# Batch 3's q and k turned by transposing transfers instead of by TensorE

## The chip, the cores and the metric

The kernel runs on one core of a Trainium2 chip. The metric is the time of one execution on the device in microseconds (us). A core has TensorE (matrix products, with a queue of its own for loading weights), VectorE, ScalarE, GpSimd and SyncE; in the profile's lines they are PE and PEld, DVE, ACT, POOL and SP. DMA transfers are issued by SyncE and GpSimd, at the end by ScalarE too.

## The reference

The inputs q, k and v have 8 batches, 8 heads, 576 positions and 64 elements; s has one number for each batch, head and position. The kernel computes causal attention with a bias from the running sum of s, and a mixer behind it:

```python
scores = scale * np.matmul(q, k.transpose(0, 1, 3, 2))
cum = np.cumsum(np.maximum(s, 0.0), axis=-1)
bias = -(cum[:, :, :, None] - cum[:, :, None, :])
scores = np.where(causal, -1000000000.0, scores + np.minimum(bias, 0.0))
attn = softmax(scores)                     # over the last axis
x = matmul(attn, v), heads side by side    # (8, 576, 512)
u = x + (x.transpose(0, 2, 1) @ U @ V).transpose(0, 2, 1)
out = u + np.maximum(u @ w_ch1, 0.0) @ w_ch2
```

For the scores, q and k of a head must lie with their 64 elements on the partitions, while they come from memory with the positions in rows. So each must be turned, and that is what the change is about.

## The kernel before

**Pairs.** The heads are taken two at a time: pair n holds two heads of batch n // 4, and there are 32 pairs (NP), four to a batch (PB). For each pair the program makes the turned q and k with the rows of the bias (a "slot" of 68 partitions: 64 of q or k and 4 of bias), then scores(n) (products at L441, exponentials on ScalarE at L459, L471 and L477, masks on VectorE at L385), then values(n) (products with v at L505; on VectorE a reciprocal at L514 and the scaled result into x_sb at L515; a transposing transfer of x_sb into xT at L522). Three slots are used in turn, so the bias rows of pair n (rows_of, L305, on SyncE) wait for the scores of pair n - 3.

**Two ways of turning.** ZB = 4 says which batches go which way. For batches 0 to 3, load(b) brings q and k of a whole batch with few large transfers on GpSimd (L132 or L137), into qk_sd0 and qk_sd1 in turn (batch b into qk_sd[b % 2]). transposes(n) turns a pair on TensorE: 16 transposes at L325, eight for each head, into two PSUM buffers of the pool pwork. Four copies (L345 from batch 2's second half on, L348 before) move them into the slot, by parity of the run; copies() puts a few of them on ScalarE. For batches 4 to 7, load_pair(n) brings one pair with four transfers on GpSimd (L124), turn_pair(n) turns it with one transposing transfer on SyncE (L365) into a landing place, and part_pair(n) copies it into the slot with one VectorE copy for each head (L375). There are three landing places: a tile of its own ("turned"), a part of qk_sd0 behind the pairs, and the front of qk_sd1.

**The order.** The loop at L1255 takes n from 8 on. Step n does, as far as each exists: loads of a later batch, turn_pair(n + 3), load_pair(n + 7), the turning of pair n + 1 (transposes or part_pair), scores(n), values(n - 1), loads of v (L188). Between the pieces, step_fill() puts pieces of the mixer: chanmix, with products at L675 into pwork, ScalarE's ReLU at L1052, sums at L711 and L260 on VectorE, products at L733, additions at L747; seqmix(b), with products at L535 that read all of batch b's x_sb, goes between the pieces of step 4b + 5. The order on TensorE and GpSimd is that of the program (L1333). On VectorE, ScalarE and SyncE a scheduler may move instructions; placed() (L907) ties a copy at L375 to the VectorE instruction that the program has before it, and `after(tc, last_sp(), x_turned[-1])` (L369) ties a turn on SyncE behind the latest transposing transfer of x.

**What waits for what on the queues.** Each engine takes its instructions in order. A turn waits until its pair is loaded and its landing place has been copied out; a load of a later pair into the same place waits for the turn. pwork is a pool of four PSUM buffers that the transposes, parts of the scores, values and the mixer take in turn.

Of the kernel before, what the change touches and what calls it, by code (L numbers as in the profile page):

```python
# [19 lines left out]
def after(tc, ins, prev):  # L20
    tc.add_manual_dep(
        ins,
        prev.name,
        mybir.DependencyInfo(mybir.DependencyClass.NoSync, mybir.DependencyReason.DATA),
        reason="in_program_order",
    )
# [15 lines left out]
def kernel(  # L42
# [23 lines left out]
    NP = BH // 2  # L66
    PB = NP // B
# [2 lines left out]
    KA = D + 4  # L70
    NF = FF // 128
    FT = 2
    ZB = 4
    TR, RT = 96, 6

    consts = ctx.enter_context(tc.tile_pool(name="consts", bufs=1))
# [35 lines left out]
    def of_pair(n):  # L112
        return qk_sd[ZB % 2][:TR, ds(n % PB * QK // PB, QK // PB)].rearrange(
            "p (c t two d) -> p c t two d", c=2, t=RT, two=2
        )
# [4 lines left out]
    def load_pair(n):  # L120
        b, hp = divmod(n, PB)
        for hh in range(2):
            for c, src in enumerate((q, k)):
                nc.gpsimd.dma_start(  # L124
                    out=of_pair(n)[:, c, :, hh, :],
                    in_=src[b, 2 * hp + hh].rearrange("(t p) d -> p t d", p=TR),
                )
# [54 lines left out]
    def load_v(b, parts=range(5)):  # L182
        vt = v_slot(b)
        if 0 < b < 3:
            init_v(nc.gpsimd, vt)
        for t in parts:
            rows_t = 128 if t < 4 else 64
            nc.gpsimd.dma_start(  # L188
                out=vt[:rows_t, t, :, 0:D],
                in_=v[b, :, ds(t * 128, rows_t), :].rearrange("h p d -> p h d"),  # L190
            )
# [161 lines left out]
    landings = [consts.tile([128, 2 * S], BF16, name="turned")]  # L353
    landings += [qk_sd[ZB % 2][:, ds(QK, 2 * S)], qk_sd[(ZB + 1) % 2][:, 0 : 2 * S]]

    def landing(n):
        return landings[(n - ZB * PB) % 3]

    x_turned = []

    def last_sp():
        return [ins for ins in list(nc.cur_bb.bb.instructions) if ins.engine == E.SP][-1]

    def turn_pair(n):
        nc.sync.dma_start_transpose(  # L365
            out=landing(n).rearrange("p (a m) -> p a m", m=TR),
            in_=of_pair(n).rearrange("p c t two d -> p (c t two d)"),
        )
        after(tc, last_sp(), x_turned[-1])  # L369

    def part_pair(n):
        rows_of(n)
        for hh in range(2):
            placed(
                lambda: nc.vector.tensor_copy(  # L375
                    slot_of(n)[0:D, hh, 0 : 2 * S], landing(n)[ds(hh * D, D)]
                )
            )
            yield
# [57 lines left out]
    def scores(n, pT, spins=()):  # L437
        slot = slot_of(n)

        def mm(dst, hh, j, lo, hi):  # L440
            nc.tensor.matmul(  # L441
                dst,
                lhsT=slot[0:KA, hh, ds(S + j * 128, 128)],
                rhs=slot[0:KA, hh, lo:hi],
                start=True,
                stop=True,
            )

        tail = None
        if spins:  # L450
            tail = pwork()
            spin(spins[0], tail)
        for hh in range(2) if n > 0 else ():
            near = pscore()
            for j in range(4):
                mm(near[:, ds(j * 128, 128)], hh, j, j * 128, j * 128 + 128)
            mm(near[:, 512:960], hh, 0, 128, S)
            mm(near[:, 960:1024], hh, 3, 512, S)
            nc.scalar.activation(pT[:, hh, 0:1024], near, EXP, scale=scale)  # L459
            if n >= PB:  # L460
                mask(pT[:, hh, 0:512].rearrange("p (a b) -> p a b", a=4), 4, 128)
            if spins:
                spin(spins[1 + hh], tail)
            yield
        mid, tail = pscore(), tail if spins else pwork()
        for hh in range(2):
            mm(mid[:, ds(hh * 512, 320)], hh, 1, 256, S)
            mm(mid[:, ds(hh * 512 + 320, 192)], hh, 2, 384, S)
            if spins and hh == 0:
                spin(spins[3], tail)  # L470
        nc.scalar.activation(  # L471
            pT[:, :, 1024:1536], mid.rearrange("p (a b) -> p a b", a=2), EXP, scale=scale
        )
        yield
        for hh in range(2):
            mm(tail[:, ds(hh * 64, 64)], hh, 4, 512, S)
        nc.scalar.activation(  # L477
            pT[:, :, 1536:1600],
            tail[:, 0:128].rearrange("p (a b) -> p a b", a=2),
            EXP,  # L480
            scale=scale,
        )
        if n >= PB:
            mask(pT[:, :, 1536:1600], 2, 64)
        yield
# [606 lines left out]
    def step_fill():  # L1092
        pace[0] += pace[1]
        if pace[0] < 16:
            return
        pace[0] -= 16
        if NG - 3 in expanded and not ps_tail:
            return
        while fill:
            if next(fill[0], fill) is not fill:  # L1100
                return
            fill.pop(0)

    def run(gen):
        for _ in gen:
            step_fill()
# [5 lines left out]
    def fill_with(n):  # L1112
        per, pace[1] = pace[1], 16
        for _ in range(n):
            step_fill()
        pace[1] = per


    def pT_of(n):
        if n < PB + 3:  # L1120
            return pTs[n % 2] if n % PB < 2 else pT_early[n % PB - 2]
        return pTs[(n + 1) % 2]

    def step(*gens):
        for gen in gens:
            next(gen, None)
# [85 lines left out]
    def load(b):  # L1212
        alloc_qk(b)
        for h in range(0, H, 4 if b == 2 else H):
            load_qk(b, h, 4 if b == 2 else H)
# [39 lines left out]
    for n in range(2 * PB, NP + 2):  # L1255
        b, hp = divmod(n, PB)
        if hp == 0 and b + 1 < ZB:
            load(b + 1)
        if ZB * PB <= n + 3 < NP:
            turn_pair(n + 3)  # L1260
        if n + 5 == ZB * PB:
            for m in range(ZB * PB, (ZB + 1) * PB):
                load_pair(m)
        if (ZB + 1) * PB <= n + 7 < NP:
            load_pair(n + 7)
        mixing = seqmix(b - 1) if hp == 1 and b > FT else iter(())
        if b == B:
            fill_with(3)
            for _ in range(3):
                step(mixing)  # L1270
                fill_with(2)
        if n > 2 * PB and n + 1 < NP:
            for at, _ in enumerate((transposes if n + 1 < ZB * PB else part_pair)(n + 1)):
                step_fill()
                if at == 0:
                    step(mixing)
        if 2 * PB + 1 < n < NP:
            for at, _ in enumerate(scores(n, pT_of(n))):
                step_fill()
                if at == 1:  # L1280
                    step(mixing)
        for _ in mixing:
            fill_with(1)
        if hp == 1 and FT < b < B:
            fill.append(chanmix(b - 1))
            pace[1] = 12 if b < 6 else 10
        if 2 * PB < n <= NP:
            run(values(n - 1, pT_of(n - 1)))
        if 2 <= b < B - 1:
            if b + 1 < ZB:  # L1290
                load_v(b + 1, range(5 if hp == 0 else 0))
            else:
                load_v(b + 1, ((0, 1), (2,), (3,), (4,))[hp])
# [70 lines left out]
```

## Time and profile before

| | us |
|---|---|
| median of 3 runs | 353.72 (353.6 to 353.72) |
| the profiled execution | 353.81 |
| its span | 352.1 |
| TensorE busy | 341.3 |
| VectorE busy | 264.3 |
| ScalarE busy | 207.5 |
| GpSimd busy | 113.2 |

The granted TensorE clock was 0.999 in this execution. The span is what the trace covers; 1.7 us of the execution lie around it. A group's line gives the source line, engine and operation, output and inputs, shapes and count, then the busy time and the mean length in ns, then the idle time of the engine before them and what ended it. A line of the chain gives start, length and the work that the end of the kernel hung on. A line of a timeline gives start, length, engine, line, operation and tiles, and in brackets the idle time before it with what ended that. A transfer's line shows when it was issued, not when its data came.

### The profile page before, as it was taken

How to read it: one execution, taken by the hardware profiler on the slowest of the kernel's cores; microseconds unless marked ns; L12 is line 12 of the kernel's file. 1: busy time of each engine (PE TensorE's matmuls, PEld its weight loads, DVE VectorE, ACT ScalarE, POOL GpSimd, SP SyncE). 2: the span in 40 equal slices, each digit the busy share in tenths (PEclk: the TensorE clock that was granted, in tenths of full speed). 3: DMA queues.
4: the chain of work that ended last, by engine and by line, in shares of the span. 5: the costliest groups of instructions: out<-in, count | busy, mean ns of one | idle time of the engine just before them, and what ended most of it. 6: DMA issues, size and time to landing. Idle time of an engine off the chain costs nothing.

```text
span 352.1 us, 9157 instructions
## 1 busy us (share of the span) xinstructions
PE 341.3 (97%) x3735; PEld 248.6 (71%) x3770; DVE 264.3 (75%) x584; ACT 207.5 (59%) x314; POOL 113.2 (32%) x158
## 2 busy tenths in 40 slices
PE   8999999999999999999999999999899999999996
PEld 4685566666588756885688567866587558888885
DVE  8686776778797857985699549974888588775774
ACT  4795975747763577347743785368562545675710
POOL 8898373534724047244634456000000000000000
PEclk9999999999999999999999999999999999999999
DMA  7999999999949999999999999784034333010022
GB/s 101 154 198 205 182 185 135 145 146 141 132 41 120 176 141 128 133 120 199 136 133 123 203 135 149 125 156 93 0 69 101 89 67 85 30 61 32 30 91 89
DMA packets 163713, 42.06 MB, mean 119 GB/s; under 512 B 148312, under 2 KB 162040, under 8 KB 163672
## 3 DMA queue, kind: packets, MB, share of 16 engines
q0 software_dynamic: 101744, 18.45, 77.8%
q1 hardware_dynamic: 61640, 22.83, 35.4%
q8 instruction: 29, 0.48, 0.6%
q10 hardware_dynamic: 288, 0.20, 0.2%
q14 instruction: 12, 0.10, 0.1%
HBM read 37.25 MB, written 9.70 MB: 133 GB/s over the span
## 4 chain that ended last, share of the span: by engine, by line
PE 82%; DVE 10%; ACT 5%; issue 3%; DVEq 0%; ACTq 0%
PE pwork L675 23%; PE pwork L733 13%; PE quarter L733 10%; PE pscore L441 9%; PE pwork L505 7%; PE parts L963 6%; PE pwork L694 3%; PE pwork L325 2%; ACT pT L459 2%; DVE uT L560 2%; DVE slot L348 2%; ACT hT L1052 2%; PE pscore L216 1%; DVE slot L711 1%; PE pscore L402 1%
## 5 line engine op out<-in xcount | busy, mean ns | idle before, releaser
L675 PE MATMUL pwork<-uT,w_sb 128*128 128x512 bf16 x405 | 104.4, 379 | 2.5 <-ACT hT L1052 0.9
L1052 ACT ACTIVATE hT<-pwork 128x512 bf16<-128x512 f32 x108 | 65.4, 611 | 37.0 <-PE pwork L675 36.1
L459 ACT ACTIVATE pT<-pscore 128x1024 bf16<-128x1024 f32 x56 | 56.5, 1031 | 47.3 <-PE pscore L441 47.2
L675 PEld LDWEIGHTS <-w_sb 128*128 128x128 bf16 x448 | 38.8, 98 | 37.9 <-issue 1.3
L441 PE MATMUL pscore<-slot 68*128 68x320 bf16 (+1 forms) x500 | 55.4, 246 | 0.6 <-ACT hT L459 0.3
L441 PEld LDWEIGHTS <-slot 68*128 68x128 bf16 x564 | 41.8, 97 | 18.0 <-issue 0.9
L733 PEld LDWEIGHTS <-hT 128*128 128x128 bf16 x496 | 46.6, 98 | 7.1 <-DVE uT L560 0.5
L385 DVE TENSOR_TENSOR pT<-pT,keep 128x512 bf16<-128x512 bf16 (+1 forms) x81 | 28.6, 354 | 28.0 <-ACT pT L459 22.2
L124 POOL DMA_DIRECT2D qk_sd<-in_q_dram x32 | 23.7, 739 | 69.0 <-DMA qk_sd<-qk_sd 43.5
L188 POOL DMA_DIRECT2D v_slot<-in_v_dram x40 | 34.1, 864 | 19.6 <-PE pwork L505 7.8
L505 PEld LDWEIGHTS <-pT 128*128 128x128 bf16 x870 | 32.5, 98 | 7.1 <-issue 1.4
L505 PE MATMUL pwork<-v_slot,pT 128*128 128x65 bf16 x870 | 35.8, 193 | 0.9 <-DVE slot L348 0.6
L515 DVE TENSOR_TENSOR x_sb<-pwork,rec 128x320 bf16<-128x320 f32 x64 | 31.1, 488 | 1.3
L471 ACT ACTIVATE pT<-pscore 128x1024 bf16<-128x1024 f32 x29 | 30.4, 1047 | 2.6 <-PE pscore L441 2.4
L733 PE MATMUL pwork<-w_sb,hT 128*128 128x256 bf16 x240 | 30.1, 273 | 0.0
L348 DVE COPY slot<-pwork 64x576 bf16<-64x576 bf16 x30 | 24.1, 803 | 7.0 <-PE pwork L325 6.6
L733 PEld LDWEIGHTS <-slot 128*128 128x128 bf16 x256 | 24.1, 98 | 4.2 <-issue 1.2
L124 POOL DMA_DIRECT2D qk_sd<-in_k_dram x32 | 23.7, 741 | 2.3 <-PE pwork L441 1.2
L514 DVE RECIPROCAL rec<-pwork 128x5 f32<-128x5 f32 x64 | 12.1, 191 | 14.2 <-PE pwork L505 13.5
L733 PE MATMUL pwork<-w_sum,slot 128*128 128x256 bf16 x160 | 20.1, 272 | 0.4 <-DVE o_sb L747 0.4
L733 PE MATMUL quarter<-w_sb,hT 128*128 128x256 bf16 x144 | 18.0, 273 | 0.3 <-DVE uT L560 0.3
L976 DVE TENSOR_TENSOR hT<-pT,parts 128x512 bf16<-128x512 f32 x16 | 10.8, 684 | 6.3 <-PE parts L963 3.6
(166 smaller groups left out, 519.3 us busy)
## 6 DMA issues: line engine op xcount, KB each, us to landing
out_dram<-o_sb SPq DMA_DIRECT2D x34, 256.0 KB
v_slot<-in_v_dram POOLq DMA_DIRECT2D x32, 128.0 KB, 7.1
w_sb<-in_moe_w_ch_dram POOLq DMA_DIRECT2D x4, 1024.0 KB, 12.6
qk_sd<-in_q_dram POOLq DMA_DIRECT2D x32, 72.0 KB, 4.0
qk_sd<-in_k_dram POOLq DMA_DIRECT2D x32, 72.0 KB, 4.3
qk_sd<-in_q_dram POOLq DMA_DIRECT2D x4, 288.0 KB, 12.9
qk_sd<-in_k_dram POOLq DMA_DIRECT2D x4, 288.0 KB, 11.7
qk_sd<-in_q_dram POOLq DMA_DIRECT2D x4, 144.0 KB, 5.3
```

The source lines that it names most:

```text
L124: nc.gpsimd.dma_start(out=of_pair(n)[:, c, :, hh, :], in_=src[b, 2 * hp + hh].rearrange("(t p) d -> p t d", p=TR),)
L188: nc.gpsimd.dma_start(out=vt[:rows_t, t, :, 0:D], in_=v[b, :, ds(t * 128, rows_t), :].rearrange("h p d -> p h d"),)
L348: copies(n, hh, par)(in_turn[:, :, :, :, par], src.rearrange("p c t m -> p c m t"))
L385: nc.vector.tensor_tensor(dst, dst, keep[:, :, 0:w].to_broadcast([128, n_tiles, w]), op=ALU.min)
L441: nc.tensor.matmul(dst, lhsT=slot[0:KA, hh, ds(S + j * 128, 128)], rhs=slot[0:KA, hh, lo:hi], start=True, stop=True,)
L459: nc.scalar.activation(pT[:, hh, 0:1024], near, EXP, scale=scale)
L471: nc.scalar.activation(pT[:, :, 1024:1536], mid.rearrange("p (a b) -> p a b", a=2), EXP, scale=scale)
L505: nc.tensor.matmul(po[:, i, :], lhsT=pT[:, hh, ds(place(j, i), 128)], rhs=vt[:, j, h, :], start=(j == 0), stop=(j == i), skip_group_check= ...
L515: nc.vector.tensor_tensor(x_sb[:, hp, :, ds(hh * D, D)], po[:, :, 0:D], rec.to_broadcast([128, 5, D]), op=ALU.mult,)
L675: nc.tensor.matmul(f1, lhsT=w1_sb[:, kt, ds(nf * 128, 128)], rhs=u[:, kt, :], start=(kt == 0), stop=(kt == 3),)
L733: nc.tensor.matmul(acc[:, i, :], lhsT=a[:, kt, ds(i * 128, 128)], rhs=b[:, kt, :], start=(begin and i == 0 and kt == 0), stop=(kt == HF - ...
L1052: nc.scalar.activation(hT[:, nf, :], f1, RELU)
```

## The change

ZB goes from 4 to 3: batch 3 (pairs 12 to 15) takes the second way. Its q and k are no longer loaded by load(3) but pair by pair into qk_sd1; the landing places behind the pairs and at the front move to qk_sd1 and qk_sd0. The load of a pair is now issued in turn_pair, right behind the turn that frees its place (pair n + 4 behind turn n). The turns of the first three pairs get places of their own: pair 12's at the end of step 10's scores, pair 13's at the start of step 11, pair 14's at the end of step 11's scores; pair 15's follows at the start of step 12, and from there on turn_pair(n + 3) comes at step n as before. The four pairs of batch 3 are loaded at step 8. As b + 1 < ZB no longer holds for batch 3, its v is loaded in pieces over steps 8 to 11, as that of the later batches is.

```diff
-    ZB = 4
+    ZB = 3
...
         after(tc, last_sp(), x_turned[-1])
+        if n + PB < NP:
+            load_pair(n + PB)
...
-        if ZB * PB <= n + 3 < NP:
+        if ZB * PB + 3 <= n + 3 < NP:
             turn_pair(n + 3)
-        if n + 5 == ZB * PB:
+        if n + 1 == ZB * PB:
+            turn_pair(n + 2)
+        if n + 4 == ZB * PB:
             for m in range(ZB * PB, (ZB + 1) * PB):
                 load_pair(m)
-        if (ZB + 1) * PB <= n + 7 < NP:
-            load_pair(n + 7)
         mixing = seqmix(b - 1) if hp == 1 and b > FT else iter(())
...
                 if at == 1:
                     step(mixing)
+        if n + 2 in (ZB * PB, ZB * PB + 1):
+            turn_pair(2 * n + 4 - ZB * PB)
         for _ in mixing:
             fill_with(1)
```

In the built program this takes 64 transposes with their weight loads from TensorE; on VectorE 14 copies at L345 go and 8 at L375 come, and one of pair 14's two stands ahead of the masks of pair 12's scores; on ScalarE 2 copies go; on GpSimd 2 transfers at L132 go and 16 at L124 come; on SyncE 4 transposing transfers come. The remaining order of TensorE and ScalarE is the same; on SyncE a few output transfers stand before a transposing transfer of the mixer that they stood behind.

## The prediction

> **What bounds the kernel now.** I read the page's busy shares first, then the chain of waits in the stretch that the change touches (74 to 120 us), then VectorE's, SyncE's and GpSimd's timelines beside it, and last the groups by form for the durations.
>
> ```profile
> PE 341.3 (97%) x3735; PEld 248.6 (71%) x3770; DVE 264.3 (75%) x584; ACT 207.5 (59%) x314; POOL 113.2 (32%) x158
> PE 82%; DVE 10%; ACT 5%; issue 3%; DVEq 0%; ACTq 0%
> ```
>
> TensorE (PE) is busy 97% of the span and holds 82% of the chain, so a TensorE instruction that goes away is worth its length, unless another engine is next in line at that place. The chain where batch 3 is handled says where that is so:
>
> ```profile
> 87.32 0.28 PE pwork L325 x8
> ...
> 88.66 0.26 PE pwork L325 x8
> ...
> 95.29 0.62 DVE slot L711
> 95.91 0.41 DVE x_sb L515
> 96.32 0.05 issue
> 96.37 0.39 PE pwork L675
> ...
> 103.20 0.26 PE pwork L325 x8
> 103.46 0.88 PE pwork L733 x8
> 104.34 0.49 PE pwork L535 x20
> 104.83 0.27 PE pwork L325 x8
> ...
> 116.38 0.28 PE pwork L325 x8
> 116.66 0.88 PE pwork L733 x8
> 117.54 0.26 PE pwork L325 x8
> ```
>
> Columns are start, length, work. The groups at L325 are the transposes of batch 3: pair 12 at 87.3 and 88.7, pair 13 at 95.5 (not on the chain), pair 14 at 103.2 and 104.8, pair 15 at 116.4 and 117.5. They are on the chain, but around 95 us the chain runs through VectorE: TensorE waits for L515 to empty a PSUM buffer. And L535 at 104.34 reads the x_sb that VectorE finished only at 104.39 (L515 twice, 103.50 for 0.89). VectorE sits right behind TensorE there.
>
> **TensorE, removed.** 64 transposes in groups of 8 or 16. By the chain: 0.28 + 0.26 (pair 12), 0.26 + 0.27 (14), 0.28 + 0.26 (15); pair 13's 16 cost 0.52, the length that the chain shows for pair 11's equal group at 80.04. Sum 2.13 us, 33 ns each. The row of all these matmuls gives a mean of 199 ns, but they overlap; what counts is the distance between them. Eight PSUM buffers also leave the rotation of four (pwork), and with them the 0.16 us of idle before 96.37. Together 2.3 us.
>
> The Trainium skill, page "TensorE: Matmul & The Clock Gate", section "Part 4: PE-mode transpose", gives about 275 ns for one transpose in a kernel's context. By that figure the 64 would be worth 17.6 us, an estimate from that page; the chain shows 33 ns apart, and the measurement decides.
>
> **VectorE and ScalarE.** The copies out of PSUM go, one copy per head from the landing place comes.
>
> ```profile
> L345 DVE COPY slot<-pwork 64x576 bf16<-64x576 bf16 x20 | 9.0, 452 | 0.3
> L375 DVE COPY slot<-qk_sd 64x1152 bf16<-64x1152 bf16 x20 | 9.2, 460 | 0.2
> L375 DVE COPY slot<-turned 64x1152 bf16<-64x1152 bf16 x12 | 6.1, 509 | 0.1
> ```
>
> Batch 3 has 16 copies at L345, 14 on VectorE (6.3 us) and 2 on ScalarE (pair 14; 1.3 us, free, as ScalarE waits there). Eight at L375 cost 3.9 us. VectorE saves 2.4 us. What matters is how much of that comes before L535: pairs 12 and 13 cost 1.87 each before and 1.02 and 0.92 after, and in the new order one copy of pair 14 (0.46) stands ahead of it, so VectorE arrives 1.34 us earlier. TensorE arrives 0.54 + 0.52 + 0.26 = 1.32 earlier. The two match, so TensorE's gain survives only if VectorE does not wait: each further microsecond of waiting, once VectorE's own idle time is used up, costs about one.
>
> **The new waits.** The copies of pairs 12 to 14 wait for a turned pair to land. Behind the waiting copies in VectorE's queue stand the masks of the same step's scores, the reciprocals and L515 (which free pwork), and the sums at L711; TensorE waits for all of these. SyncE gets four more turns. Each comes behind a transposing transfer of x (L522), since the code chains it there: pair 12 behind the one at 83.14, pairs 13 and 14 both behind the one at 88.22, pair 15 behind the one at 96.34. The rows after them (L305) move back by 1.3 to 4 us; the ones issued at 84.58 are for pair 13's scores at 105.97, so that is hidden by 20 us. How long a turn takes is read off GpSimd, which waits for it before it loads the next pair into the place:
>
> ```profile
> 118.78 1.30 SPq L365 DMA_TRANSPOSE qk_sd<-qk_sd  x1
> ...
> 126.16 2.33 SPq L365 DMA_TRANSPOSE qk_sd<-qk_sd  x1
> ```
>
> ```profile
> 123.06 0.73 POOL L124 DMA_DIRECT2D qk_sd<-in_q_dram  x1 [8.38 <-DMA qk_sd<-qk_sd]
> ...
> 134.34 0.73 POOL L124 DMA_DIRECT2D qk_sd<-in_q_dram  x1 [7.53 <-DMA qk_sd<-qk_sd]
> ```
>
> That is 4.3 us from issue to release with nothing loading beside it, 8.2 us just after a pair's load had started. For pair 12: issued at about 84.5, lands 88.8 to 92.7, wanted at 88.7. VectorE has 2.2 us of idle between there and 94.5 (0.79 + 0.49 + 0.69 + 0.23 in its timeline), so 0 to 1.8 of net waiting. Pair 13: issued at 89.6, lands 93.9 to 97.8, wanted at about 95.7, so 0 to 2.1. Pair 14, right behind it: 95.3 to 99.5, wanted at 97.2; if 13 was late it adds little. As these waits overlap, I bound the sum at 0 and 2.3 and take 0.5, near the quiet end: the loads of pairs 16 to 19, which in the profile fill GpSimd's queue from 74.5 to 95.1, now come only after the turns of 12 to 15, so the DMA engines have nothing but one pair's load and one piece of v beside the turns of 13 and 14. Pair 15 is issued near 98 and wanted at 117, free.
>
> **GpSimd.** Two loads at L132 (1.83 and 1.81 us) become 16 at L124 (0.74 each), 11.8 us from 59.0, so until about 71. As many rows move as before. Batch 3's v now comes in pieces, three behind these loads, the fourth behind pair 16's, the last behind those of 17 and 18, which wait for the turns of 13 and 14: issued at about 102, landing 7 us later (the page's median), near 109. It is read by values(12) at 113.5: hidden, with 4 us to spare; past that, TensorE waits. The loads of 16 to 19 move by 10 to 15 us; pair 16 is turned at 105.9, after its load.
>
> **Sum.** -2.3 (TensorE and the idle) + 0.5 (VectorE's wait) = -1.8 us. The profiled execution took 353.81 with a span of 352.1, so 1.7 lie around it; it would come to a span of 350.3 and 352.0. The median of the runs is 353.72, and from it I say 351.9. Past 118 us nothing takes the gain back that I can see: no copy at L375 waits for a transfer in the list of waits, and pair 16 lands at 110.9 for a copy at 124.2.
>
> **Rivals.**
> 1. The turns of 13 and 14 take the 8 us that they take beside a load, and VectorE's wait of about 2.3 eats the gain: -2.3 + 2.3 = 0, 353.7 (353.0 to 354.4). For it: pair 16's load starts right when pair 12 has landed, just as the load at 123.06 did before the turn at 126.16. Against: of the first eight turns four land within 5.1 us. Chance 0.22.
> 2. Slower: SyncE's queue comes late to pair 12. The transposing transfer of uT (L1039), two places ahead of it, held the queue for 7 us in the profile:
>
> ```profile
> 74.93 7.03 SPq L1039 DMA_TRANSPOSE u_sd<-uT  x1
> ```
>
> It held it because batch 3's loads and v ran beside it; they now go out in 16 pieces at the same time. If the backlog grows by another 7 us, pair 12 lands at 96 instead of 89, VectorE stands 7.3 less its 2.2 of idle = 5.1, and the time is 353.7 - 2.3 + 5.1 = 356.5. It decides from a wait of 3.0 us in all (0.7 over no change). Against: v's last pieces and the next pairs' loads no longer follow in GpSimd's queue, so the backlog should end sooner. Chance 0.17. The Trainium skill speaks for this side: page "VectorE: DVE Perf Modes", "The three transpose paths", puts a 128x128 block at 1309 ns by DMA and 390 ns by TensorE, and its rules for authors prefer TensorE where PSUM will do. Taken block by block, a pair's 12 blocks would need 15.7 us, an estimate from that page, and VectorE would stand still for longer than this rival says; the 4.3 us above speak against it.
> 3. More than I say: no wait, and the stretch to 113.5, where the chain runs through VectorE, is shorter by what pair 14's copies after 105 save (0.91 before, 0.46 after): 2.3 + 0.45 = 2.7, 351.0. Chance 0.03.
>
> My forecast (waits of 0 to 1.2 us; 351.4 to 352.6) has 0.58. About 0.2%, 0.7 us, is what a measurement of this kernel can tell from no change. Faster by more: 0.58 + 0.03 + 0.03 (the near edge of rival 1) = 0.64; within: 0.17; slower: 0.17 + 0.02 = 0.19. The range runs from 350.9, just below rival 3, to 354.8, past the bound of 2.3 on the wait; it leaves out rival 2 and some edges, about 0.19.
>
> **What would show it.** Right: L325 has 192 matmuls, no L345 row for batch 3, GpSimd's load for pair 16 is released by pair 12's turn before 90, VectorE shows little idle before the L375 copies near 88 to 98, and L535 of seqmix(2) starts near 103. Wrong: idle at VectorE before L375 "<-DMA turned" or "<-DMA qk_sd" of over 2 us, and L535 at 104 or later; or values(12) waiting for v.

## The result, and the profile after

| | changed kernel, us | kernel before, us | ratio, 95% interval |
|---|---|---|---|
| first comparison | 351.39 (350.83 to 352.77) | 353.66 | 0.9930 (0.9908 to 0.9952) |
| second | 351.65 (351.20 to 351.69) | 353.54 | 0.9941 (0.9929 to 0.9953) |
| third | 351.36 (350.90 to 354.85) | 353.43 | 0.9948 (0.9931 to 0.9965) |

The change makes the kernel faster, by 1.9 to 2.3 us in the medians; the forecast was 351.9, 1.8 below before. The first profile of the changed kernel was of a disturbed run (its span is 501.4 us, at a granted clock of 0.653), so "after" is here the profiled execution of the second comparison: 351.69 us, a span of 350.0 and a granted clock of 1.000. Lines from 370 on stand two higher in it: L377 is the copy from the landing place, L517 the multiplication into x_sb, L537 the product of seqmix, L713 and L735 sums and products of the mixer.

The busy times and the shares of the chain, from its page:

```profile
PE 339.2 (97%) x3672; PEld 246.5 (70%) x3706; DVE 261.3 (75%) x578; ACT 206.3 (59%) x312; POOL 120.8 (35%) x172
PE 78%; DVE 11%; ACT 5%; issue 4%; DMA 1%; DVEq 0%; ACTq 0%; POOLq 0%
```

TensorE is busy for 2.1 us less (341.3 before) and its records are 63 fewer; at the transposes' line (L325) they are 192 where they were 256. The chain of waits, in the stretch where before had the transposes of pair 14 around L535 (start, length, work):

```profile
97.42 0.61 DVE slot L377
...
102.73 0.86 DVE x_sb L517 x2
103.60 0.04 issue
103.64 0.29 PE pwork L537 x5
103.93 0.88 PE pwork L735 x8
```

Before, the chain ran through TensorE from 96.4 to 104.8 and only brushed VectorE. Now it runs through VectorE from 93.8 to 103.6, with pair 14's first copy (97.42) in it, and comes back to TensorE at the last five matmuls of seqmix(2). The timelines show both sides, first VectorE's copies of pairs 12, 13 and 14, then TensorE (in brackets, where there is one, the idle time and what ended it):

```profile
88.86 1.01 DVE L377 COPY slot<-turned 64x1152 bf16<-64x1152 bf16 x2
...
95.79 0.92 DVE L377 COPY slot<-qk_sd 64x1152 bf16<-64x1152 bf16 x2
...
97.34 0.69 DVE L377 COPY slot<-qk_sd 64x1152 bf16<-64x1152 bf16 x1
```

```profile
102.45 0.53 PE L537 MATMUL pwork<-U_sb,x_sb 128*128 128x32 bf16 x15
103.64 0.29 PE L537 MATMUL pwork<-U_sb,x_sb 128*128 128x32 bf16 x5 [0.66 <-DVE x_sb L517]
```

No copy has a bracket: in this trace none waited for a landing. TensorE waits 0.66 us for x_sb. Why the landings are in time is in the timelines of SyncE and of GpSimd:

```profile
75.08 3.99 SPq L1041 DMA_TRANSPOSE u_sd<-uT  x1
...
81.94 1.38 SPq L365 DMA_TRANSPOSE turned<-qk_sd  x1
...
89.77 3.18 SPq L365 DMA_TRANSPOSE qk_sd<-qk_sd  x2
```

```profile
86.51 0.74 POOL L124 DMA_DIRECT2D qk_sd<-in_q_dram  x1 [10.34 <-DMA turned<-qk_sd]
...
96.27 0.76 POOL L124 DMA_DIRECT2D qk_sd<-in_q_dram  x1 [5.76 <-DMA qk_sd<-qk_sd]
```

The transposing transfer of the mixer took 3.99 us on SyncE in place of 7.03, so the turn of pair 12 went out at 81.94 and not at about 84.5; GpSimd was released by it at 86.51, 4.6 us later. Pairs 13 and 14 went out at 89.77; pair 13's copies at 95.79 did not wait, so it had landed within 6.0 us, and GpSimd's load behind it began 6.5 us after issue.

The margin is thin, though. In the eight traces of changed variants that issue pair 12's turn at 81.4 to 82.0, GpSimd's next load begins 3.9 to 7.4 us after it, and in three of the eight a copy of pair 13 or 14 does wait for its landing, for 0.17 to 0.19 us.

**Where the time went, place by place.** This execution runs 0.15 us later than that of before from the first reciprocal of values on. With that taken off, the first reciprocal of values(10) comes 0.75 us earlier than before, of values(11) 0.94, of values(12) 1.31, of values(13) 1.86, of values(16) 1.66, of values(20) 1.99, and the last matmul 1.99. So nearly all is won between 87 and 118 us, and at the end it is still there.

### The profile page after: what moved, and what is told of

It reads as the page before. It is cut to its first block, busy times and chain, and to the rows that moved or that the text cites. A ratio compares the mean times of both kernels' runs of the same rounds, so it can differ in the third digit from the quotient of the medians.

```text
span 501.4 us, 9050 instructions
## 1 busy us (share of the span) xinstructions
PE 491.9 (98%) x3672; PEld 313.8 (63%) x3706; DVE 267.2 (53%) x578; ACT 218.5 (44%) x312; POOL 119.9 (24%) x172
## 4 chain that ended last, share of the span: by engine, by line
PE 97%; issue 1%; DMA 1%; ACT 0%; DVE 0%; POOLq 0%
PE pwork L677 27%; PE pwork L735 18%; PE pscore L443 12%; PE quarter L735 10%; PE pwork L507 8%; PE parts L965 6%; PE pwork L696 4%; PE pwork L325 2%; PE pscore L404 2%; PE pscore L677 1%; PE pwork L965 1%; DMA qk_sd<-in_q_dram 1%; PE pwork L216 1%; PE pwork L537 1%; PE parts L826 1%
## 5 line engine op out<-in xcount | busy, mean ns | idle before, releaser
L677 PE MATMUL pwork<-uT,w_sb 128*128 128x512 bf16 x406 | 150.0, 510 | 3.7 <-issue 1.2
L461 ACT ACTIVATE pT<-pscore 128x1024 bf16<-128x1024 f32 x56 | 56.4, 1023 | 76.3 <-PE pscore L443 73.5
L677 PEld LDWEIGHTS <-w_sb 128*128 128x128 bf16 x448 | 48.0, 117 | 64.2 <-issue 59.8
L443 PE MATMUL pscore<-slot 68*128 68x320 bf16 (+1 forms) x500 | 77.3, 308 | 0.0
L443 PEld LDWEIGHTS <-slot 68*128 68x128 bf16 x564 | 54.9, 119 | 31.9 <-issue 24.9
L735 PEld LDWEIGHTS <-hT 128*128 128x128 bf16 x496 | 57.2, 119 | 21.9 <-issue 2.2
L124 POOL DMA_DIRECT2D qk_sd<-in_q_dram x40 | 29.3, 732 | 142.8 <-DMA qk_sd<-qk_sd 71.9
L507 PEld LDWEIGHTS <-pT 128*128 128x128 bf16 x870 | 44.0, 111 | 9.8 <-issue 8.5
L507 PE MATMUL pwork<-v_slot,pT 128*128 128x65 bf16 x870 | 46.8, 218 | 0.0
L735 PE MATMUL pwork<-w_sb,hT 128*128 128x256 bf16 x240 | 42.8, 345 | 0.0
L735 PEld LDWEIGHTS <-slot 128*128 128x128 bf16 x256 | 29.2, 118 | 10.9 <-issue 0.9
L517 DVE TENSOR_TENSOR x_sb<-pwork,rec 128x320 bf16<-128x320 f32 x64 | 31.1, 488 | 1.3
L124 POOL DMA_DIRECT2D qk_sd<-in_k_dram x40 | 29.3, 732 | 2.5 <-DMA qk_sd<-in_q_dram 1.8
L735 PE MATMUL pwork<-w_sum,slot 128*128 128x256 bf16 x160 | 28.6, 346 | 0.0
L735 PE MATMUL quarter<-w_sb,hT 128*128 128x256 bf16 x144 | 26.2, 349 | 0.0
L696 PE MATMUL pwork<-w_sb,hT 128*128 128x512 bf16 x58 | 22.1, 517 | 0.7 <-issue 0.2
```

The source lines that it names most:

```text
L124: nc.gpsimd.dma_start(out=of_pair(n)[:, c, :, hh, :], in_=src[b, 2 * hp + hh].rearrange("(t p) d -> p t d", p=TR),)
L443: nc.tensor.matmul(dst, lhsT=slot[0:KA, hh, ds(S + j * 128, 128)], rhs=slot[0:KA, hh, lo:hi], start=True, stop=True,)
L507: nc.tensor.matmul(po[:, i, :], lhsT=pT[:, hh, ds(place(j, i), 128)], rhs=vt[:, j, h, :], start=(j == 0), stop=(j == i), skip_group_check= ...
L517: nc.vector.tensor_tensor(x_sb[:, hp, :, ds(hh * D, D)], po[:, :, 0:D], rec.to_broadcast([128, 5, D]), op=ALU.mult,)
L677: nc.tensor.matmul(f1, lhsT=w1_sb[:, kt, ds(nf * 128, 128)], rhs=u[:, kt, :], start=(kt == 0), stop=(kt == 3),)
L696: nc.tensor.matmul(f2, lhsT=hT[:, nf, ds(i * 128, 128)], rhs=w2_sb[:, nf, :], start=False, stop=(nf == NF - 1), skip_group_check=True,)
```

## Experiments

Two theories stood at first. Mine: TensorE's 64 transposes are the gain, and VectorE's queue takes a part of it back at seqmix(2). The rival: the gain comes from something that moved with them (SyncE's shorter queue, copies taken off VectorE), or is set by the landings. The changed kernel as it is ran along as the measure.

> The changed kernel as it is, for a profile at full clock. Theory (TensorE's 64 transposes are the gain, the landings come in time): 351.4 us again; 192 matmuls at the transposes' line, VectorE waits less than 1 us in all before the copies of the turned pairs 12 to 14, the product of seqmix(2) that read x_sb starts near 103 us (104.3 before). Rival (part of the gain is eaten by waits for landings, so that it could have been larger): 1 to 2.3 us of idle on VectorE before those copies, seqmix(2) at 103.5 or later.

It took 351.65 us, ratio 0.9941 (0.9929 to 0.9953).

**The transposes put back.** Into the changed kernel, for pairs 12 to 15, at the place of the copy:

```diff
     def part_pair(n):
         rows_of(n)
+        if n < 4 * PB:
+            idle = pwork().bitcast(BF16)[:, : 2 * 4 * TP].rearrange(
+                "p (c t m) -> p c t m", c=2, t=4
+            )
+            for c in range(2):
+                for t2 in range(4):
+                    nc.tensor.transpose(
+                        idle[:, c, t2, :], busy[:TP, ds(t2 * 128, 128)],
+                        identity[:TP, :TP])
```

(The same stands in front of the second copy.)

> The changed kernel with 64 idle transposes of a constant tile on TensorE, at the places and in the PSUM buffers where batch 3's stood; nobody reads them, and all other queues are as in the changed kernel. Theory (the gain is TensorE's time): all of it comes back, 353.4 to 353.8 us. Rival (the gain is VectorE's and ScalarE's, who have fewer copies): 351.2 to 351.8, no change against the changed kernel.

Measured: 352.96 us, ratio 0.9987 (0.9978 to 0.9995); that is below the expected 353.4 to 353.8, so not all of the gain came back. Its chain of waits (L382 are the transposes, L548 is seqmix, L688 a product of the mixer that stands between two groups of transposes):

```profile
87.23 1.04 PE pwork L688 x4
...
95.28 0.52 PE pwork L382 x16
...
102.47 0.26 PE pwork L382 x8
...
103.62 0.69 PE pwork L548 x20
104.31 0.27 PE pwork L382 x8
```

The groups have the lengths that before showed, the chain lies on TensorE again, and the wait in seqmix(2) is gone. Of the 1.89 us by which this comparison's medians differ, 1.31 go back; in the traces, net of the start, 1.8 of 1.99. So the transposes on TensorE are most of the gain, and SyncE, GpSimd and VectorE as changed, without them, are worth 0.2 to 0.6 us.

**VectorE's copies twice.** In the changed kernel each copy of pairs 12 to 15 is made twice, eight more in all, five of them ahead of seqmix(2):

```diff
-            placed(
+            for _ in range(2 if n < 4 * PB else 1):
+                placed(
...
```

> The changed kernel with each VectorE copy of a turned pair of batch 3 made twice: 8 copies of about 0.47 us more, 2.3 us of them ahead of seqmix(2). Theory (VectorE sits right behind TensorE there, and each microsecond of its delay costs about one): 353.0 to 354.0 us. Rival (VectorE has slack in the changed kernel): within 0.7 us of 351.4.

Measured: 354.54 us (352.49 to 357.17), ratio 1.0033 (1.0010 to 1.0055); again, beside a later experiment, 354.59 (352.58 to 356.66), ratio 1.0025 (1.0003 to 1.0046). Both are above the expected 353.0 to 354.0.

> The kernel with the copies twice once more, unchanged, as the measure for the one with 16 more matmuls in the wait, on the same chip. Expected: as before, most runs near 354.4 us with a mean clock of 0.995, some near 352.7 with 1.0.

The loss of 2.9 us is more than the wait explains. TensorE's timeline (L538 is seqmix), and below it the stretches from 104 to 110 us (after the five engines' busy times with their counts: the granted clock of TensorE, the DMA share, GB/s):

```profile
104.58 0.29 PE L538 MATMUL pwork<-U_sb,x_sb 128*128 128x32 bf16 x5 [2.00 <-DVE x_sb L518]
```

```profile
104.00:106.00 2.00, 1.42 (x12) 1.09 (x13) 1.93 (x6) 0.00 (x0) 1.91 (x3) 0.73 2.15 139
106.00:108.00 2.00, 2.00 (x15) 1.49 (x14) 0.55 (x1) 0.69 (x1) 2.00 (x4) 0.50 1.72 156
108.00:110.00 2.00, 2.00 (x20) 1.68 (x19) 1.22 (x3) 1.49 (x3) 0.75 (x1) 0.92 1.67 200
```

The wait has grown by 1.34 us, from 0.66 to 2.00; and behind it the granted clock is 0.73, 0.50 and 0.92 for 2 us each, which costs 2 x (0.27 + 0.50 + 0.08) = 1.7 us, as much as 3.4 us at half clock. Together 3.0. Not every run has the second part: of these 12, ten have a mean clock of 0.989 to 0.995 (354.23 to 357.17 us) and two of 1.000 (352.49 and 352.83, 1.0 above the changed kernel). Two of the ten, 357.11 and 357.17, have 0.989 and 0.990, about twice the drop.

**Is it the idle time that brings the clock down?** 16 matmuls that nobody needs fill that wait:

```diff
-        up = pwork()[:, 0:128]
+        room = pwork()
+        up = room[:, 0:128]
         for dt in range(4):
+            if (b, dt) == (2, 3):
+                spin(16, room[:, 256:512])
```

> The kernel with the copies twice, and 16 more matmuls in TensorE's queue (of a constant tile, 128x256, into a part of the same PSUM tile that nobody reads), ahead of the last five of seqmix(2), where TensorE waits 2.0 us for x_sb. At 0.117 us apart, as in the group of 16 at L735, they take 1.9 us and so fit into the wait; VectorE, ScalarE and the queues are unchanged. They keep TensorE busy, and do no useful work. Theory (10 of 12 runs of the kernel with the copies twice lose 1.7 us more than the copies cost, because TensorE's granted clock falls to about 0.5 for 4 us after that wait): no drop in the granted clock from 104 to 110 us, all runs near 352.7 us (352.3 to 353.1). Rival 1 (the clock falls for another reason than the idle time): 354.4, with a drop, as without the matmuls. Rival 2 (the matmuls cost time themselves): 354.4 or more at a full clock.

Measured: 353.15 us (352.64 to 353.70), ratio 0.9990 (0.9981 to 0.9998), beside 354.59 without them on the same chip. TensorE's timeline (L216 are the 16, L541 is seqmix), and the same stretches:

```profile
102.30 1.91 PE L216 MATMUL pwork<-busy 128*128 128x256 bf16 x16
104.43 0.29 PE L541 MATMUL pwork<-U_sb,x_sb 128*128 128x32 bf16 x5 [0.22 <-DVE x_sb L518]
```

```profile
104.00:106.00 2.00, 1.78 (x24) 1.39 (x23) 1.93 (x5) 0.00 (x0) 2.00 (x4) 1.00 1.69 110
106.00:108.00 2.00, 2.00 (x24) 1.70 (x21) 1.08 (x3) 1.92 (x3) 2.00 (x3) 1.00 1.53 160
108.00:110.00 2.00, 2.00 (x22) 1.53 (x21) 1.52 (x5) 1.15 (x3) 0.45 (x1) 1.00 1.71 99
```

x_sb is as late as before (the last five start at 104.43 and 104.58), yet the clock stays at 1.00, in all 11 runs (mean 0.999 or more); without the 16, on the same chip, eight of 12 lie at 0.995 or less. Work without use makes this variant 1.4 us faster. So the idle time is the cause of the drop. The median lies just above the expected 352.3 to 353.1, and 0.3 above that of the four runs without the 16 that kept a full clock (352.58 to 353.10): the 16 may cost a little themselves, as rival 2 had it, but far less than the drop costs.

**The turns alone, a first try.** Into the kernel before, four spare turns at the places of those of pairs 12 to 15, reading what pairs 16 to 19 load:

```diff
+    def turn_spare(n):
+        nc.sync.dma_start_transpose(
+            out=landings[n % 2].rearrange("p (a m) -> p a m", m=TR),
+            in_=of_pair(n).rearrange("p c t two d -> p (c t two d)"))
+        after(tc, last_sp(), x_turned[-1])
...
-        if n + 5 == ZB * PB:
+        if n + 6 == ZB * PB:
```

> The kernel before with four more transposing transfers, of pairs 16 to 19 into landing places that are free then, at the places in SyncE's queue where the changed kernel turns pairs 12 to 15; nothing reads them. It prices the transfers alone (SyncE's time and the DMA engines'). Theory (hidden): 353.3 to 354.1 us. Rival (they hold up the loads and the bias rows behind them): 354.4 us or more.

Measured: 370.75 us, ratio 1.0487 (1.0464 to 1.0509). This does not price the turns: for them the loads of pairs 16 to 19 were put one step earlier, into the buffer that pair 11's q and k still lie in, so that pair 11's transposes come behind these loads (and turn what the loads bring). TensorE's timeline has 15.1 of the 17.2 us lost in one row (behind it the granted clock is still 0.50 until 100 us):

```profile
94.80 0.76 PE L325 MATMUL pwork<-identity,qk_sd 72*128 72x72 bf16 x10 [15.09 <-issue]
```

**The turns alone, better made.** The same four, reading v, which is in place, with the loads left as they are:

```diff
+    def turn_spare(n):
+        nc.sync.dma_start_transpose(
+            out=landings[n % 2].rearrange("p (a m) -> p a m", m=TR),
+            in_=v_slots[1 if n == 19 else 2].rearrange("p a b c -> p (a b c)")[:TR, 0:1536])
+        after(tc, last_sp(), x_turned[-1])
...
+        if n in (11, 12):
+            turn_spare(2 * n - 5)
...
+        if n in (10, 11):
+            turn_spare(2 * n - 4)
```

> The kernel before with four spare turns (transposing transfers of one pair's size, from values that are in place to the landing places, read by nobody) at the places at which the changed kernel issues those of pairs 12 to 15; nothing else is changed, and TensorE still transposes pairs 12 to 15. It prices the four transfers and their places in SyncE's queue alone. Theory (the transfers are hidden: what they delay in SyncE's queue has 20 us to spare): 353.2 to 354.0, within 0.2% of before. Rival (the transposing transfers disturb the loads, the rows or the transfers of x, and the changed kernel wins in spite of that): 354.4 or more.

Measured: 353.51 us, ratio 0.9999 (0.9990 to 1.0008). Four more transposing transfers and their places in SyncE's queue cost nothing that can be measured.

**The wait of 0.66 us.** If it is VectorE's own queue, one copy less ahead of x_sb shortens it:

```diff
     def part_pair(n):
...
+            if (n, hh) == (14, 0):
+                after(tc, last_dve(), x_made[-1])
             yield
...
+            x_made.append(last_dve())
```

The last line stands in values(), behind the multiplication into x_sb. Nothing else is moved, on any engine.

> The changed kernel with one instruction moved: pair 14's first copy from the landing place (0.46 us) stands behind values(11)'s last multiplication into x_sb in VectorE's queue, no longer in front of the masks of pair 12's scores. All other queues stay as they are. Theory (the 0.66 us for which TensorE waits in seqmix(2) is VectorE's own queue, and not a landing): VectorE is 0.45 us earlier there, the wait shrinks to about 0.2, and the time is 351.2 (350.9 to 351.4) where the changed kernel takes 351.65. Rival (something else ends the wait, or the time is given back at the next meeting of the two engines): 351.5 to 351.9.

Measured: 351.16 us (350.82 to 351.64), ratio 0.9935 (0.9923 to 0.9947). TensorE's timeline (L545 is seqmix):

```profile
102.15 0.78 PE L545 MATMUL pwork<-U_sb,x_sb 128*128 128x32 bf16 x20
```

The 20 matmuls stand in one group, with no wait. The last matmul of the program comes 0.56 us earlier than in the changed kernel (net of the start). This run and that of the changed kernel were on different chips. Both were run side by side once more:

> The changed kernel once more, unchanged, as the measure for the one with pair 14's first copy moved, on the same chip. Expected: 351.3 to 351.7 us.

> The changed kernel with pair 14's first copy behind values(11)'s last multiplication, once more, on the same chip as the changed kernel. Theory (its trace has no wait of TensorE in seqmix(2) any more, and its last matmul ends 0.56 us earlier, once the different start of the first work is taken off): 0.5 us below the changed kernel, 350.9 to 351.2. Rival (the two single medians differ by chance): within 0.2 us of the changed kernel.

Measured: 351.36 us, ratio 0.9948 (0.9931 to 0.9965), for the changed kernel, and 351.15 us (350.31 to 351.65), ratio 0.9930 (0.9917 to 0.9942), with the copy moved. The wait is 0.78 us in the one trace and 0.16 in the other. So the theory of the wait holds: it was VectorE's queue. On the same chip the medians differ by 0.21 us, less than the 0.5 of the theory and close to the 0.2 that the rival gave to chance; the intervals overlap. It is faster than the kernel before beyond doubt. Against the changed kernel only the traces speak for it: each of the two with the copy moved ends earlier than each of the two without, by 0.42 to 0.92 us net of the start, but those two without differ by 0.36 themselves. One of the changed kernel's 12 runs here (354.85 us) has a mean clock of 0.994, a drop of about the size seen above; no trace of that run was kept, so where it fell is not known. None of the ten with the copy moved has one.

**A landing that is late.** The turn of pair 12 issued one step later:

```diff
         if n + 1 == ZB * PB:
+            turn_pair(n + 1)
             turn_pair(n + 2)
...
-        if n + 2 in (ZB * PB, ZB * PB + 1):
-            turn_pair(2 * n + 4 - ZB * PB)
+        if n + 1 == ZB * PB:
+            turn_pair(n + 3)
```

> The changed kernel with the turn of pair 12 issued one step later, right ahead of those of pairs 13 and 14, at about 89.8 us in place of 81.9. It makes the landing late, which in the changed kernel it is not, and so prices the wait that the prediction was afraid of. Theory (each microsecond that VectorE waits, past its own idle time, costs about one): pair 12 lands 4.6 us after issue, at 94.4; VectorE, which has the first mask of pair 11 in front of the copies now, is done with that at 91.2 and waits 3.2 us, of which 0.2 to 0.4 is covered: 354.4 us (353.5 to 356.3, the upper end with a landing after 6.5 us). Rival 1 (TensorE has other work to do meanwhile, the wait is hidden): 352.5 or less. Rival 2 (three turns in a row hold each other up, and pairs 13 and 14 wait again): 356.5 or more.

Measured: 353.18 us (352.62 to 354.81), ratio 0.9998 (0.9985 to 1.0012): below the expected 353.5 to 356.3. VectorE's timeline and TensorE's:

```profile
92.87 0.92 DVE L377 COPY slot<-turned 64x1152 bf16<-64x1152 bf16 x2 [2.12 <-DMA turned<-qk_sd]
```

```profile
104.73 0.29 PE L537 MATMUL pwork<-U_sb,x_sb 128*128 128x32 bf16 x5 [1.71 <-DVE x_sb L517]
```

VectorE's copies begin 3.5 us after the turn's issue at 89.33, so the wait is 2.12 and not 3.2. GpSimd's load behind the same turn begins at 93.42, 4.1 us after issue: the 4.6 that was expected had been read off GpSimd, which begins later than VectorE. x_sb is ready 1.5 us later than in the changed kernel (net of the start), since some of VectorE's idle time behind the copies took the rest; the nine runs at a full clock have a median of 353.04, 1.4 above the changed kernel (which ran on another chip). The other three (354.47 to 354.81) have the drop of the clock too. So a landing 2 us late eats most of the gain, as the prediction's rival 1 said, and theory's one for one holds for what is left after the idle time.

## Why the prediction was right, point by point

**TensorE, 2.13 us and 0.16 of idle: right.** L325 has 192 matmuls, TensorE's busy time fell by 2.1, and putting the transposes back returned 1.3 (medians) to 1.8 us (traces), net of the wait in seqmix(2), which was gone then. 33 ns for each was the measure, not the 199 ns of the row. The 275 ns of the Trainium skill (page "TensorE: Matmul & The Clock Gate", "Part 4: PE-mode transpose") are the length of one transpose, like the 199 here, and no price of a removal: by them the 64 would be worth 17.6 us, an estimate that the runs do not bear out.

**VectorE and TensorE match at L535: partly wrong.** The prediction had both arrive 1.3 us earlier. Before:

```profile
103.50 0.89 DVE L515 TENSOR_TENSOR x_sb<-pwork,rec 128x320 bf16<-128x320 f32 x2
104.17 0.66 PE L535 MATMUL pwork<-U_sb,x_sb 128*128 128x32 bf16 x20
```

After (TensorE's row is above, at 102.45):

```profile
102.70 0.89 DVE L517 TENSOR_TENSOR x_sb<-pwork,rec 128x320 bf16<-128x320 f32 x2
```

Net of the start, TensorE came 1.87 earlier (104.17 to 102.45) and VectorE's last L517 ended 0.95 earlier (104.39 to 103.59).

VectorE's 0.39 less than the predicted 1.34 comes from three mis-sized terms. Pair 12's saving of 0.85 was taken as a whole, but VectorE is idle behind these copies, for ScalarE (0.90, 0.49 and 0.23 us) and TensorE (0.69), so what counts there is how much earlier ScalarE's scores come, 0.75. Pair 14's copy takes 0.61 of the queue (97.34 to the next start at 97.95), not 0.46. And pair 13's copies save 0.69 by the starts of the rows around them, not the 0.95 that their lengths gave; of this 0.26, half (0.13) comes back behind them.

TensorE's 0.55 more than said lies between the same rows. It holds the 0.16 of idle, which the prediction left out of this step, and 0.18 more behind that idle time, where the first matmul of L675 took 0.39 us on the chain (0.22 in the chain with the transposes put back, where that wait is gone). The other 0.21 lies around pair 12's transposes. In the chain of before, the four matmuls between their two groups took longer than the four behind:

```profile
87.63 1.04 PE pwork L675 x4
...
88.92 0.88 PE pwork L675 x4
```

With the transposes put back, the 1.04 is back as well (87.23 in that chain). So taking a group away was worth a little more than its own length here.

**The new waits, 0.5 us: the number nearly right, the cause wrong.** No copy waited for a landing. That a wait of about this size came all the same, from another cause, is luck. The 0.66 that TensorE does wait is VectorE's queue, as moving one copy showed. The landings were early because pair 12's turn went out at 81.94, not 84.5; the prediction had taken over SyncE's 7.03 us for the transfer of uT, though the loads beside it were to change. It also read the time of a turn off GpSimd, whose load begins 0.43 to 0.55 us later than the VectorE copy that waits for the same turn.

**SyncE and GpSimd hidden: right.** Four spare turns cost nothing that could be measured. GpSimd's 16 loads were done at 73.5, not 71, for they wait in between; v's last piece went out at 102.03, as said, and values(12) did not wait for it.

**The sum.** By the prediction's terms the trace would give -2.3 + 0.66 = -1.6. By the starts of the rows it closes better: TensorE's 1.87 up to seqmix(2), and 0.27 + 0.54 for the transposes behind it (pair 14's second group, and pair 15), less 0.82 in seqmix(2), where the 0.66 of waiting is joined by 0.16 for the 20 matmuls that now stand in two groups. That makes 1.86, which is what values(13) shows; the end has 1.99, and the last 0.13 I can't place. So -1.8 came near partly by luck: the gain was taken 0.39 too small and the loss 0.32 too small.

**Rival 1** (the gain eaten by a wait of 2.3 us) has the right mechanism: with a wait of 2.12, made by issuing the turn late, the ratio is 0.9998 (three of the 12 runs with the drop of the clock among them; the nine others keep 0.45 us of the gain). Its condition did not hold, for the turns of pairs 13 and 14 landed in time. **Rival 2** (SyncE's backlog grows) went the other way: the backlog shrank by 3.0 us. By the price of the Trainium skill that the prediction set beside it (page "VectorE: DVE Perf Modes", "The three transpose paths"), a turn would have taken 15.7 us, an estimate; pair 12's took 4.6. **Rival 3** (351.0) had the right side of the forecast, though not its condition: there was a wait. What the prediction lacked is the drop of the clock: with a wait near 2 us in seqmix(2), 1.7 us can come on top, which rival 2's 356.5, reckoned one for one, leaves out.

## What to carry to other kernels

Price a removed TensorE instruction by its distance to the next one in the chain, look at whether its neighbours are slower beside it, and then follow the next engine to the meeting point: a saving ahead of its idle time counts only as far as what it waits for comes earlier too. A copy that need not be early should stand behind the instruction that another engine waits for. Where TensorE's wait reaches 1.7 us, look at the granted clock behind it before you price the wait.

## What the runs showed of the hardware

- Behind waits of 1.71 to 2.46 us in seqmix(2), after 15 matmuls only 32 wide, TensorE's granted clock fell to 0.50 for about 3.4 us in the three traces with such a wait, at a cost of 1.7 us. It fell in 21 of the 36 runs of the two variants (the copies twice, taken two times, and the late turn), in four of them for about twice as long by the mean clock (0.989 to 0.990), and in none of 11 with the wait filled. Of the changed kernel's 26 runs at 350.8 to 354.9 us, one has a drop too; its traces show waits of 0.66 and 0.78. The Trainium skill, page "TensorE: Matmul & The Clock Gate", "Part 1: The HAM clock gate", has half the clock after an idle window of about 3.4 us, and calls the window free-running. The half agrees (0.50), and that some runs are spared would fit such a window; but a wait need not fill it, since 1.71 us of idle were enough here.
- The transposing transfer of uT held SyncE's queue for 6.83 to 7.03 us in the three traces where batch 3 came by two large loads, and for 3.60 to 4.30 in the nine where it came in 16 pieces. What ran beside it differs in more than the size of the pieces. In the profile of before, the large load of k, issued at 61.31, landed only 18.4 us later, near 79.7, and two pieces of v and pair 16's loads went out between 72.98 and 76.0. In the changed kernel the 16 pieces were out by 73.5, and from 76.2 to 86.5 GpSimd issued nothing. Which part lengthens the hold was not tried.
- GpSimd's load that waits for a turn began 0.43 to 0.55 us after the VectorE copy that waited for the same turn, in the four traces where both waited (92.87 and 93.42 with the late turn). Times from issue to GpSimd's load are that much longer than times to the landing as VectorE sees it.
- By GpSimd's load, pair 12's turn took 4.6 us in the changed kernel's profile, 3.9 to 7.4 in the eight traces that issue it near 82, and 4.1 where it is issued late; pair 13's, just behind a pair's load, 6.5 us.
